# Second product of chunks 1 to 5 with 20 block products in place of 14 per chunk of larger ones, x kept in DRAM, and a new written order

## The chip, the cores and the metric

The kernel runs on one core of one Trainium2 chip. Its time is the device time of one execution in microseconds (us), lower is better; "the median" is that of the executions shown. A profile is one further execution, taken by the hardware profiler. The engines are PE (TensorE: matmuls, with PEld for its weight loads), DVE (VectorE), ACT (ScalarE), POOL (GpSimd) and SP (SyncE, which issues nearly all DMAs).

## The reference

Two parts follow each other. A gated linear recurrence over 4 batches, 8 heads, 768 positions and head size 48, and then a channel MLP with layer normalisation over the 384 values of a position:

```python
for t in range(S):
    state = alpha[:, :, t, :, None] * state + np.einsum('bhd,bhe->bhde', k[:, :, t], v[:, :, t])
    y[:, :, t] = np.einsum('bhd,bhde->bhe', q[:, :, t], state)
x = y.transpose(0, 2, 1, 3).reshape(B, S, H * D)          # (4, 768, 384)
xn = (x - mean(x)) / np.sqrt(var(x) + 1e-06) * g_ln
out = x + np.maximum(xn @ w_ch1, 0.0) @ w_ch2             # w_ch1 384 x 1536, w_ch2 1536 x 384
```

Token tensors are float32; the gain and the weights come as 64-bit floats and are turned to float32 on the chip.

## The kernel before

The 768 positions are cut in 6 chunks of 128 (c = 0 to 5), and all 4 batches (b) of a chunk are worked in parallel. There are these streams of work, each a Python generator that issues one step per turn:

- `attention(c, b)`, 24 of them: logarithm and running sums of the gates (ACT, PE), scaled q and k in the tiles `qks[b]` and `eqs[b]` (DVE, POOL), transposes, masked products (`at`), the output `yps`, the copy of it to `x` (line 290), the state update with the gate row (SP moves one row to DRAM and back, lines 241 and 273), statistics, `xn`, and its transpose into `xT`.
- `take_weights(i)`, 12 pieces: 768 KB are loaded in the tiles `ws` and converted by DVE and ACT.
- `mlp()`: for chunk 0 the plain products (`hidden`, `project`, lines 337 and 349). For chunks 1 to 5 both products are replaced by block schemes that need fewer products and more sums. The first product (`hidden_product`, line 510) uses 15 block products for 18, in the order `FIRST`, twice per chunk (r = 0, 1). The second (`product`, line 404) treats two batches at a time: 7 products of 6 matmuls each in place of 8, so 14 products and 84 matmuls per chunk, each with a moving operand of 192 columns. Every matmul in float32 appears in the trace as two records of PE (two passes).
- `combine_x`, `combine_hidden` (line 390: 4 sums of 128x768 per pair of batches, on DVE), `combine_first` and `combine_weights` (lines 462 and 369, sums of blocks of the weights, on POOL, once), and `relus` (line 562, ACT).

After each product of line 404 its PSUM tile is read: by one DVE or ACT instruction of 128x192, products 5 by two; some results go on to sums on POOL (lines 413, 422, 423, 427). These PSUM tiles (`ops`, `hps`) share the tag "m" with three buffers: the fourth product must wait until the first one has been read. The result tile `ob` (three buffers) starts from `x`, which waits in SBUF in nine buffers, and `send` (line 566) writes it out.

The order of all this is written out by hand in the string `ORDER`: one letter per turn (a to x the attentions, A to L the weight pieces, M the MLP, S the sums of the weights, R relus, X `combine_x`, N `combine_hidden`). Each engine works through its own queue strictly in this order, and so does SP with its DMAs.

Of the kernel before, what the change touches and what calls it, by code (L numbers as in the profile page):

```python
# [22 lines left out]

ORDER = (
    "ababdaacbaabccaabacdacbaabadcbbbdcdAabbbdaBcCccdabAeddbcbdcffcdfeegacfcbagdhfbde"
    "adbceBeegAdhfBCfdeabdfefcAheiBeafdeagjgbecfebcfcgeegfdefdgcghhihfdcgdegCCigMhMgD"
    "DhMjEMEjFMhiDkhfMgfighFheMFFfMMIMEIhIDMgEjhMGhMgjMhgfMGiHMMGGkMMMMHeiJMkMlHJMigM"
    "IMLJilHljMejKKjiLKeLjMhhfjSigSMhMlSMglSlhgiffMKkMhMhSSSMSSSMXiXkikXSXiimjMXXXSSM"
    "MXkMMSkjMMXkMkMMSMMjMmMMjXkmMSlmiMSMMiMkMMXkMjMMMlMlmRMmMMMokSjlMlMnlMnMljnkMMMR"
    "MjnMMMMSMMmMnMMmnRMMRRMoRSkiMlpklniMkpnjmMMRMmMRpkMRMNMMNmMlMiRkmMMiNMMnloMpRMSM"  # L30
    "njNMMkplMoRMMMkMMNmjNMMlMMNNmonnMljomqMMlqMMlnXMMXMXmXnXXMXqMMMXmmXMMooMMMMpMpMn"
    "MMXMMoMoMMMrMoXMnRqoRmoMpMMrpMMMMMMpMMpRnproMMmMMmqMMMrMMMqqMsMMnMnMpJqrRnqsMorM"
    "tMMMMmqMooRppMpotsRMMtRMtMrMRqMRNMoMNMRNMMrMpRMoNsMqMspqpMoMtMMRMMMNMNMMNMMMoMpn"
    "MpNsrrnMtrpqvrquXrXXrXMquXqXsMXsrMXrMqMMXMXuMMMMrMrMLMsMtXMMstMMMtqMsstMMMMMqvRR"
    "MMvMsuMsMtuMMRMMMrMMuwMMMMRMMMvwMvqMttqMMMruRMMRMMsMMRMMMMRMssRtwtsvutxvMRNsvMNN"
    "tMvNsRtRMMMvMtMMuusMMtMMwuuMrMMwwxNxMxvrtNNMMMNMMMtxsMMMuXMXXXMvMvuuXxXXMXvXuMMM"
    "MwwXwMMxMMxMXMMMMMMuvMMxMMuMMwRxMMMwwRMvMwMMMRxuxwxwwMuxMRxvMwMMMxxMMMMMRMMvMMuM"
    "RMMMvMMMxMMRuMRMMRMMNMMMNRMMNMMvMMNMMMwwMMvwMxxRNwRMMNMNNMMMMwxMMvxMXXXXXXMMMMXX"
    "XMMMMMMMMMXMMMMMMMMXMMMMMRRMMMMMMMMMMMMMRMMRMMMMMMMMMMRRMMMRMMRMMMMMMRMNMMMNRNMM"
    "MMNMMMMMMMRMNRMNMMNMMMMNMMMMMMMM"  # L40
# [4 lines left out]
def kernel(  # L45
# [85 lines left out]
    g_col = cpool.tile([P, NF], FP32, name="g_col")  # L131
# [63 lines left out]
    eps = cpool.tile([P, 1], FP32, name="eps")  # L195
    nc.vector.memset(eps, EPS)
    least = cpool.tile([P, 1], FP32, name="least")
# [3 lines left out]
    eqs = [cpool.tile([P, NP, 2, 64], FP32, name=f"eq{b}") for b in range(B)]  # L201
    qks = [cpool.tile([P, 2, NP, 2, 64], FP32, name=f"qk{b}") for b in range(B)]
# [5 lines left out]


# [4 lines left out]
    g20 = cpool.tile([P, NF], FP32, name="g20")  # L214
# [6 lines left out]
    def attention(c, b):  # L221
        qk = qks[b].rearrange("p i a b c -> p i (a b) c")
        eq = eqs[b].rearrange("p a b c -> p (a b) c")[:, :, :D]
# [14 lines left out]
        if c + 1 < NCB:  # L238
            row = dram.tile([1, NP, P], FP32, name="row", tag="row")
            gate = work.tile([P, NP], FP32, name="gate", tag="gate", bufs=B)  # L240
            nc.sync.dma_start(row, eqs[b][P - 1:P].rearrange("o a b c -> o a (b c)"))
# [6 lines left out]
        for i in range(2):  # L248
            tps = ps.tile([R, NP, P], FP32, name="tps", tag="a", bufs=3)
            for p in range(NP):  # L250
                nc.tensor.transpose(  # L251
                    tps[:, p], qks[b][:, i, p].rearrange("p a b -> p (a b)")[:, :R], ident)
            yield
            if i == 0 or c < 2:
                nc.scalar.copy(out=qkT[:, i], in_=tps)
            else:
                nc.vector.tensor_copy(out=qkT[:, i], in_=tps)
            yield
# [30 lines left out]
        x_of[c, b] = x = work.tile([P, DM], FP32, name="x", tag="x", bufs=9)  # L289
        nc.scalar.copy(out=x, in_=yps.rearrange("p a b d -> p (a b d)"))  # L290
        yield
        if c + 1 < NCB:
            sps = ps.tile([R, NP, D], FP32, name="sps", tag="s")
            heads = list(enumerate((slice(0, 64), slice(64, R))))
            for p in range(NP):
                for i, s in heads:
                    nc.tensor.matmul(sps[s, p], qks[b][:, 1, p, i, :s.stop - s.start],  # L297
                                     vt[:, 2 * p + i], start=True, stop=True)
# [32 lines left out]

    def hidden(c, j):
# [10 lines left out]
    ops_of = {}  # L343

    def project(c, b, js):
# [6 lines left out]
        if js[-1] == NJ - 1:  # L352
            ob = work.tile([P, DM], FP32, name="ob", tag="ob", bufs=3)
            nc.vector.tensor_add(ob, ops_of.pop(b), x_of.pop((c, b)))
            nc.sync.dma_start(out[b, c * P:(c + 1) * P], ob)
# [3 lines left out]
    HJ, HM = NJ // 2, DM // 2  # L359
    win = {}  # L360

    def combine_weights():
        b11, b12 = w2[:, :HJ, :HM], w2[:, :HJ, HM:]
        b21, b22 = w2[:, HJ:, :HM], w2[:, HJ:, HM:]
        t1, t2, t4 = (t[:, :HJ * HM].rearrange("p (a c) -> p a c", c=HM) for t in spare)
        ready = win["b"] = {1: b11, 2: b21, 3: b22}
        for n, o, x, y in ((5, t1, b12, b11), (6, t2, b22, t1), (4, t4, b21, t2),
                           (7, b12, b22, b12)):
            nc.gpsimd.tensor_sub(o, x, y)
            ready[n] = o  # L370
            yield

    def quarters(c, b):
        if (c, b) not in win:
            hT = hT_of[c]
            a11, a12, a21, a22 = (hT[:, js, i] for i in (b, b + 1)
                                  for js in (slice(0, HJ), slice(HJ, NJ)))
            win[c, b] = {1: a11, 2: a12, 4: a22}, a21
        return win[c, b]

    def combine_hidden(c, b):
        ready, a21 = quarters(c, b)
        a11, a12, a22 = (ready[n] for n in (1, 2, 4))
        s2, s3, s4 = (work.tile([P, HJ, P], FP32, name=f"sum{i}", tag=f"sum{i}", bufs=1)
                      for i in range(3))
        for n, op, o, x, y in ((7, nc.vector.tensor_sub, s3, a11, a21),
                               (5, nc.vector.tensor_add, a21, a21, a22),
                               (6, nc.vector.tensor_sub, s2, a21, a11),
                               (3, nc.vector.tensor_sub, s4, a12, s2)):
# [4 lines left out]
    def product(c, b, n):  # L394

        if n == 1:
            for i in (0, 1):
                win["o", i] = work.tile([P, 2, HM], FP32, name="ob", tag="ob", bufs=3)
            u = [work.tile([P, 512], FP32, name="u", tag=f"u{i}", bufs=1) for i in range(2)]
            for i in range(4):  # L400
                win["u", i] = u[i // 2][:, i % 2 * HM:][:, :HM]
        acc = ps.tile([P, HM], FP32, name="ops", tag="m", bufs=3)
        for j in range(HJ):
            nc.tensor.matmul(acc, quarters(c, b)[0][n][:, j], win["b"][n][:, j],  # L404
                             start=(j == 0), stop=(j == HJ - 1))
        yield
        x0, x1 = (x_of[c, i].rearrange("p (s m) -> p s m", s=2) for i in (b, b + 1))
        o0, o1 = win["o", 0], win["o", 1]
        p1, u2, u3, u4 = (win["u", i] for i in range(4))
        add, add_late = nc.vector.tensor_add, nc.gpsimd.tensor_add  # L410
        if n == 1:
            nc.scalar.copy(out=p1, in_=acc)
            add_late(o0[:, 0], p1, x0[:, 0])
        elif n == 4:
            add(o1[:, 0], acc, x1[:, 0])
        elif n == 2:
            add(o0[:, 0], acc, o0[:, 0])
        elif n == 6:
            add(u2, acc, p1)
        elif n == 7:  # L420
            add(u3, acc, u2)
            add_late(o1[:, 1], u3, x1[:, 1])  # L422
            add_late(o1[:, 0], u3, o1[:, 0])
        elif n == 5:
            add(u4, acc, u2)
            add(o1[:, 1], acc, o1[:, 1])
            add_late(u4, u4, x0[:, 1])
            send(c, b + 1, o1)
        else:
            add(o0[:, 1], acc, u4)  # L430
            send(c, b, o0)
            del x_of[c, b], x_of[c, b + 1]
# [5 lines left out]
    HB, NT = B // 2, NJ // 3  # L438
# [28 lines left out]
    def combine_x(c):  # L467
# [3 lines left out]
        for i in range(2):  # L471
            t = work.tile([P, HJ, P], FP32, name=f"sum{i}", tag=f"sum{i}", bufs=1)
            t = t.rearrange("p a t -> p (a t)")
            new += [t[:, k * HB * P:(k + 1) * HB * P] for k in range(3)]
        t100, t101, t103 = (t[:, HJ * HM:][:, :HB * P] for t in spare)
        t102, m7, m8, m9, m10, m13 = new
# [15 lines left out]
    FIRST = (3, 7, 5, 10, 9, 1, 4, 14, 11, 6, 13, 2, 8, 0, 12)  # L492

    def hidden_product(c, r, n):
# [38 lines left out]
        elif n == 14:  # L533
            add(u2, acc, u2)
            add_late(c0, u0, u2)
        elif n == 6:
            add(c4, acc, c4)
        elif n == 11:
            nc.scalar.copy(out=c1, in_=acc)
            add_late(c0, c0, c1)  # L540
# [24 lines left out]
    def send(c, b, ob):  # L565
        nc.sync.dma_start(out[b, c * P:(c + 1) * P], ob.rearrange("p s m -> p (s m)"))

    def mlp():
        for c in range(NCB):
# [12 lines left out]
            for b in range(0, B, 2):  # L582
                for n in (1, 4, 2, 6, 7, 5, 3):
                    yield from product(c, b, n)

    spare = []

    def sums():
        for _ in range(3):
            spare.append(stage.tile([P, NF, 2 * P], INT64, name="ws", tag="ws")  # L590
                         .rearrange("p a c -> p (a c)").bitcast(FP32))
# [7 lines left out]
              "N": (x for c in range(1, NCB) for b in range(0, B, 2)  # L599
                    for x in combine_hidden(c, b))}  # L600
# [32 lines left out]
```

## Time and profile before

| quantity | value |
|---|---|
| median of 3 executions | 475.4 us (474.47 to 475.61) |
| the profiled execution's own time, its span | 473.87 us, 471.8 us |
| PE busy, records | 459.0 us (97%), 3712 |
| DVE busy | 327.1 us (69%) |
| POOL busy | 203.8 us (43%) |
| ACT busy | 152.0 us (32%) |
| granted PE clock | full in all slices |
| DMA | 33.84 MB, 72 GB/s mean; mean share of the 16 engines over 0.8 in the first 40 us and 0.2 or less in most slices after 85 us |

An execution's time stands about 2 us above its span. A busy PE is not PE at its peak, since the ends of matmuls are modelled; the starts of neighbouring records show what one really takes.

### The profile page before, as it was taken

The numbers are of one execution on the slowest core, as the hardware profiler recorded it, in microseconds if no ns is written. First come the engines' busy times: TensorE is split into PE (matmuls) and PEld (weight loads), VectorE is DVE, ScalarE is ACT, GpSimd is POOL, SyncE is SP. The second block draws the span as 40 slices with busy tenths as digits, with TensorE's granted clock in tenths as the row PEclk, the third lists the DMA queues.
The fourth block names the chain that finished last, engine by engine and source line by source line (L and its number), as shares of the span: only waits on it lengthen the run. The fifth ranks groups of instructions, "written<-read, shape, count | busy, mean of one in ns | idle before, by whom it ended". The sixth has DMA issues, their size and how long they took to land.

```text
span 471.8 us, 9234 instructions
## 1 busy us (share of the span) xinstructions
PE 459.0 (97%) x3712; PEld 388.5 (82%) x3712; DVE 327.1 (69%) x571; ACT 152.0 (32%) x325; POOL 203.8 (43%) x203
## 2 busy tenths in 40 slices
PE   5989999999999999999999999999999999999997
PEld 3758654566788899988899998899998899987996
DVE  4899997768456985567768378685656576675742
ACT  5676533421132631114341133351203331123300
POOL 5034010049779873127553116573214281145611
PEclk9999999999999999999999999999999999999999
DMA  8988365203112102030211320120010000000000
GB/s 267 334 234 265 78 192 173 83 23 113 52 36 67 35 18 84 8 114 18 86 35 35 100 71 17 35 85 1 33 36 1 1 1 17 18 33 2 0 35 33
DMA packets 32498, 33.84 MB, mean 72 GB/s; under 512 B 13108, under 2 KB 28596, under 8 KB 32456
## 3 DMA queue, kind: packets, MB, share of 16 engines
q1 hardware_dynamic: 31912, 33.12, 22.8%
q8 instruction: 29, 0.48, 0.4%
q10 hardware_dynamic: 544, 0.13, 0.1%
q14 instruction: 13, 0.11, 0.1%
HBM read 28.49 MB, written 4.76 MB: 70 GB/s over the span
## 4 chain that ended last, share of the span: by engine, by line
PE 90%; DMA 4%; DVE 2%; POOL 2%; ACT 2%; SPq 0%; issue 0%; POOLq 0%; DVEq 0%
PE ops L404 29%; PE hps L510 26%; PE hps L337 7%; PE ops L349 7%; PE aps L264 5%; PE yps L286 4%; PE yps L281 4%; PE tps L251 3%; PE lps L228 2%; PE sps L297 2%; PE xps L325 2%; DMA rk<-in_k_dram 2%; DMA ws<-in_moe_w_ch_dram 1%; DMA ra<-in_alpha_dram 1%; DVE w L163 1%; ACT ws L169 0%
## 5 line engine op out<-in xcount | busy, mean ns | idle before, releaser
L307 POOL TENSOR_TENSOR st<-st,gate 128x384 f32<-128x384 f32 x20 | 20.6, 1034 | 76.7 <-issue 30.6
L510 PE MATMUL hps<-sum,w 128*128 128x256 f32 x200 | 51.7, 381 | 0.0
L404 PE MATMUL ops<-w,hT 128*128 128x192 f32 x240 | 42.5, 327 | 0.0
L404 PE MATMUL ops<-w,sum 128*128 128x192 f32 x240 | 42.4, 326 | 0.0
L404 PE MATMUL ops<-ws,hT 128*128 128x192 f32 x240 | 42.3, 326 | 0.0
L562 ACT ACTIVATE hT<-hT 128x512 f32<-128x512 f32 x60 | 36.6, 632 | 16.5 <-POOL hT L548 6.6
L510 PEld LDWEIGHTS hps<-sum,w 128*128 128x128 f32 x200 | 37.1, 190 | 5.2
L404 PEld LDWEIGHTS ops<-w,hT 128*128 128x128 f32 x240 | 39.3, 190 | 0.7
L404 PEld LDWEIGHTS ops<-w,sum 128*128 128x128 f32 x240 | 39.3, 190 | 0.3
L404 PEld LDWEIGHTS ops<-ws,hT 128*128 128x128 f32 x240 | 39.3, 190 | 0.0
L268 DVE COPY_PREDICATED at<-consts,aps 128x512 f32<-128x512 int32 x48 | 32.2, 724 | 10.2 <-PE aps L264 9.9
L286 PE MATMUL yps<-rv,at 128*64 128x48 f32 x768 | 36.4, 219 | 0.0
L422 POOL TENSOR_TENSOR ob<-u,x 128x192 f32<-128x192 f32 x10 | 6.9, 686 | 67.6 <-issue 42.8
L235 POOL TENSOR_TENSOR qk<-rk,ek 128x384 f32<-128x384 f32 x24 | 26.7, 1113 | 19.5 <-ACT ek L232 19.5
L286 PEld LDWEIGHTS yps<-rv,at 128*64 128x64 f32 x768 | 33.0, 137 | 1.3 <-issue 0.7
L529 POOL TENSOR_TENSOR hT<-hT,u 128x512 f32<-128x512 f32 x10 | 12.8, 1284 | 48.6 <-DVE u L528 48.5
L337 PE MATMUL hps<-xT,w 128*128 128x512 f32 x72 | 32.6, 598 | 0.0
L349 PE MATMUL ops<-w,hT 128*128 128x384 f32 x96 | 32.3, 488 | 0.0
L510 PE MATMUL hps<-xT,w 128*128 128x256 f32 x120 | 31.2, 383 | 0.0
L251 PE MATMUL tps<-consts,qk 128*112 128x128 f32 x192 | 29.2, 281 | 1.5 <-DVE at L268 1.0
L264 PE MATMUL aps<-qkT 48*128 48x128 f32 x384 | 28.6, 285 | 1.5 <-DVE at L268 0.8
L251 PEld LDWEIGHTS tps<-consts,qk 128*112 128x112 f32 x192 | 22.8, 137 | 8.8 <-issue 4.1
(127 smaller groups left out, 956.2 us busy)
## 6 DMA issues: line engine op xcount, KB each, us to landing
ws<-in_moe_w_ch_dram SPq DMA_DIRECT2D x12, 768.0 KB
ra<-in_alpha_dram SPq DMA_DIRECT2D x24, 192.0 KB
rk<-in_k_dram SPq DMA_DIRECT2D x24, 192.0 KB
rq<-in_q_dram SPq DMA_DIRECT2D x24, 192.0 KB
rv<-in_v_dram SPq DMA_DIRECT2D x24, 192.0 KB
out_dram<-ob SPq DMA_DIRECT2D x24, 192.0 KB
row<-eq SPq DMA_DIRECT2D x20, 2.0 KB
gate<-row SPq DMA_DIRECT2D x20, 2.0 KB
```

Of the source, the lines that this page charges most:

```text
L235: nc.gpsimd.tensor_mul(qk[:, 1, :, :D], raws.pop(("k", c, b)), ek)
L251: nc.tensor.transpose(tps[:, p], qks[b][:, i, p].rearrange("p a b -> p (a b)")[:, :R], ident)
L264: nc.tensor.matmul(aps[i][:, p], qkT[rows, 1, p], qkT[rows, 0, p], start=True, stop=True)
L268: nc.vector.copy_predicated(out=at[:, i], data=aps[i], mask=mask.unsqueeze(1).broadcast_to([P, NP, P]))
L281: nc.tensor.matmul(yps[s, p].rearrange("p a b -> p (a b)"), qkT[:, 0, p, s], sts[b][:R, p].rearrange("p a b -> p (a b)"), start=True, stop ...
L286: nc.tensor.matmul(yps[s, p, i], at[:, i, p, s], vt[:, 2 * p + i], start=(c == 0), stop=(c == 0 or i == 1))
L307: nc.gpsimd.tensor_mul(st, st, gate.unsqueeze(2).broadcast_to([P, NP, 2 * D]))
L337: nc.tensor.matmul(hps, w1[:, f, j * P:(j + 1) * P], xT_of[c][:, f], start=(f == 0), stop=(f == NF - 1))
L349: nc.tensor.matmul(ops_of[b], hT_of[c][:, j, b], w2[:, j], start=(j == 0), stop=(j == NJ - 1))
L404: nc.tensor.matmul(acc, quarters(c, b)[0][n][:, j], win["b"][n][:, j], start=(j == 0), stop=(j == HJ - 1))
L510: nc.tensor.matmul(acc[:, i], w, b, start=True, stop=True)
L562: nc.scalar.activation(out=x, in_=x, func=AFT.Relu)
```

## The change

Per chunk 1 to 5 the second product is computed for all 4 batches at once. Its left side is cut in 4 x 3 blocks (batches by thirds of the 12 row blocks of w2), its right side in 3 x 2 (thirds by halves of the columns), and a scheme with 20 products of 4 matmuls takes the place of 24. Per chunk these are 80 matmuls for 84, each of the same shape.

- `combine_hidden` has 16 sums of 128x512 per chunk (before: 8 of 128x768). `combine_weights` has 13 sums of 128x768 (before: 4 of 128x1152); four of the results go to a new tile `more`.
- Per chunk, PSUM is read by 24 DVE and 4 ACT instructions of 128x192 (before: 14 and 2), and POOL has 10 sums of 128x192 (before: 8).
- `x` has three buffers; each x is written to DRAM (`kept`, a new step of `attention`) and read back into `ob` (four buffers, new stream `outputs`, letter O). These are 48 more DMAs of 192 KB on SP.
- To make room, `eqs` and `qks` of batches 2 and 3 lie in `more` and are used for chunks 0 and 1 alone, where `more` is not needed yet; from chunk 2 on two `eqs` and three `qks` (b % 2, b % 3) serve all batches. Temporary results of `combine_x` move from `ws` to the `sum` tiles.
- The order of products begins with those whose left blocks need no sum: `SECOND` with 3, 18, 10, 14, and `FIRST` now with 11.
- `ORDER` is a new string.

```diff
-    eqs = [cpool.tile([P, NP, 2, 64], FP32, name=f"eq{b}") for b in range(B)]
-    qks = [cpool.tile([P, 2, NP, 2, 64], FP32, name=f"qk{b}") for b in range(B)]
+    more = cpool.tile([P, 4, NJ // 3 * DM // 2], FP32, name="more")
+    shared = more.rearrange("p i m -> p (i m)")[:, :4 * NP * P]
+    eqs = [cpool.tile([P, NP, 2, 64], FP32, name=f"eq{b}") for b in range(2)]
...
+    def eq_of(c, b):
+        return eqs[b if c < 2 else b % 2]
+    def qk_of(c, b):
+        return qks[b if c < 2 else b % 3]
...
-        x_of[c, b] = x = work.tile([P, DM], FP32, name="x", tag="x", bufs=9)
+        x = work.tile([P, DM], FP32, name="x", tag="x", bufs=3)
         nc.scalar.copy(out=x, in_=yps.rearrange("p a b d -> p (a b d)"))
         yield
+        x_of[c, b] = kept = dram.tile([P, DM], FP32, name="kept", tag="kept", bufs=4 * B)
+        nc.sync.dma_start(kept, x)
+        yield
...
+    def outputs():
+        for c in range(NCB):
+            for b in range(B):
+                ob_of[c, b] = ob = work.tile([P, DM], FP32, name="ob", tag="ob", bufs=B)
+                nc.sync.dma_start(ob, x_of.pop((c, b)))
+                yield
+    def send(c, b):
+        nc.sync.dma_start(out[b, c * P:(c + 1) * P], ob_of[c, b])
...
     def combine_weights():
...
+        for ns, op, o, x, y in (
+                ((8,), add, t8, b[1], b[5]), ((12, 18), sub, t12, b[4], b[5]),
+                ((1, 19), sub, t1, b[2], b[3]), ((9,), sub, t9, b[1], b[3]),
+                ((6,), add, n6, t9, b[5]), ((), add, b[3], b[0], b[4]),
+                ((3,), sub, b[5], b[3], b[2]), ((16,), sub, b[3], b[3], t8),
+                ((2,), add, n2, t9, b[4]), ((5,), add, n5, t9, b[2]),
+                ((10,), sub, n10, b[0], n5), ((0,), sub, n0, t8, b[2]),
+                ((13,), sub, n13, t8, b[4])):
...
+    def combine_hidden(c):
+        a, ready = blocks_of(c)
+        n0, n2, n6, n9, n5, n13 = (
+            work.tile([P, NT, P], FP32, name=f"sum{i}", tag=f"sum{i}", bufs=1) for i in range(6))
+        add, sub = nc.vector.tensor_add, nc.vector.tensor_sub
+        for n, op, o, x, y in (
+                (15, add, a[1], a[0], a[1]), (None, sub, n6, a[2], a[5]),
...
+                (None, add, n5, n5, a[6]), (7, sub, n5, n5, n13)):
+            op(o, x, y)
+            ready[n] = o
+            yield
+    SECOND = (3, 18, 10, 14, 15, 11, 2, 19, 0, 1, 6, 12, 5, 9, 8, 4, 17, 13, 7, 16)
+    def product(c, n):
...
+        acc = ps.tile([P, HM], FP32, name="ops", tag="m", bufs=3)
+        lhs, rhs = blocks_of(c)[1][n], win["b"][n]
+        for j in range(NT):
+            nc.tensor.matmul(acc, lhs[:, j], rhs[:, j], start=(j == 0), stop=(j == NT - 1))
+        yield
...
+        elif n == 18:
+            sub(o(1))
+            sub(o(3))
...
+        elif n == 13:
+            add(q4)
+            late(o(5), q4)
+            late(o(5), g, "sub")
+            late(r8, q4, "sub")
+            late(o(7), r8)
+            late(o(6), r8)
         elif n == 7:
+            add(o(5))
+            send(c, 2)
         else:
+            add(o(6))
+            send(c, 3)
...
-    FIRST = (3, 7, 5, 10, 9, 1, 4, 14, 11, 6, 13, 2, 8, 0, 12)
+    FIRST = (11, 3, 7, 5, 10, 9, 1, 4, 14, 6, 13, 2, 8, 0, 12)
...
             add(u2, acc, u2)
             add_late(c0, u0, u2)
+            add_late(c0, c0, c1)
...
             nc.scalar.copy(out=c1, in_=acc)
-            add_late(c0, c0, c1)
```

Here `add` and `sub` of `product` are DVE instructions that read the PSUM tile, `late` is a POOL instruction, and `o(k)` is half k % 2 of the result tile of batch k // 2.

## The prediction

> **What bounds the kernel now.** I read the page first (busy shares, chain), then PE's waits, then the chain in order of time over the last 60 us, then the product stages as windows.
>
> ```profile
> span 471.8 us, 9234 instructions
> PE 459.0 (97%) x3712; PEld 388.5 (82%) x3712; DVE 327.1 (69%) x571; ACT 152.0 (32%) x325; POOL 203.8 (43%) x203
> PE 90%; DMA 4%; DVE 2%; POOL 2%; ACT 2%; SPq 0%; issue 0%; POOLq 0%; DVEq 0%
> ...
> PE lps L228 <- ACT la L225: 5.4, 3, 4.3
> PE tps L251 <- DVE at L268: 1.0, 2, 0.6
> PE hps L510 <- DVE hT L553: 1.0, 1, 1.0
> ```
>
> PE idles for 471.8 - 459.0 = 12.8 us: 8.5 before 40 us (31.52 of 40 busy there), 1.0 in one place near the end, and 3.3 behind the last matmul. From 40 us on PE is one unbroken queue, so what PE has to do is the time, as long as the other engines keep ahead of it.
>
> ```profile
> 414.02 6.06 PE hps L510 x28
> 420.10 0.70 DVE hT L531
> 420.93 1.27 POOL hT L532
> 422.20 1.42 POOL hT L535
> 423.69 1.28 POOL hT L540
> 425.04 1.27 POOL hT L545
> 426.42 1.27 POOL hT L548
> 427.69 1.24 POOL hT L549
> 428.95 0.70 DVE hT L553
> 429.70 11.49 PE hps L510 x52
> 441.19 27.32 PE ops L404 x168
> ```
>
> This is the chain's end, start and length in us. 168 records of line 404 take 27.32 us: 0.1626 us each. The POOL rows are the 1.0 us wait: six sums without a gap, then L553, whose read sets a PSUM buffer free. In earlier chunks attention work lies between and hides this.
>
> ```profile
> 168.35:203.15 34.80, 34.80 (x313) 33.76 (x312) 22.16 (x43) 6.95 (x17) 14.66 (x14) 1.00 0.13 40
> 243.30:278.97 35.67, 35.67 (x332) 34.63 (x332) 24.43 (x48) 7.11 (x18) 10.04 (x13) 1.00 0.17 51
> 316.00:351.60 35.60, 35.60 (x317) 34.31 (x315) 23.91 (x46) 6.56 (x17) 9.15 (x12) 1.00 0.11 38
> 385.70:414.00 28.30, 28.30 (x179) 28.23 (x178) 19.11 (x38) 4.55 (x12) 7.02 (x10) 1.00 0.06 20
> ...
> L390 DVE TENSOR_TENSOR sum<-hT x20: 947/959/2002, 166.0 to 456.2; 128x768 f32<-128x768 f32 x20
> ```
>
> The windows are the second-product stages of chunks 1 to 4 (window, mean length; then busy PE, PEld, DVE, ACT, POOL; clock; DMA). PE is full; DVE is at 64, 68, 67 and 68%. The last line gives minimum, median and maximum ns of a sum of `combine_hidden`.
>
> **The sum, part by part**, against the profiled execution (473.87 us; its span 471.8 and 2.1 around it). The median shown, 475.4, lies 1.5 above it, so I carry the difference over.
>
> *Matmuls.* Per chunk 84 become 80, two records each: 5 x 4 x 2 = 40 records fewer, of the same shape: 40 x 0.1626 = -6.5 us. All of it is on PE's queue. The product boundaries rise from 14 to 20 a chunk, but 12, 24, 72 and 168 records in a row have taken 1.95, 3.90, 11.70 and 27.32, so a boundary costs nothing by itself.
>
> *DVE in the product stages.* Reads of PSUM: 24 x 0.354 (the 128x192 rows, 0.348 to 0.356) in place of 14: +3.5 us a chunk. Sums: a 128x256 sum takes 0.42, a 128x768 one 0.95 undisturbed, so 128x512 lies at 0.685; the 40 rows of L390 together are 43.2 us, 1.08 each, 14% over 0.95, so 0.78. 16 x 0.78 - 8 x 1.08 = +3.9. Together +7.4 a stage, while PE's share falls by 1.3: 29.6 of 33.5, 31.8 of 34.4, 31.3 of 34.3 and 26.5 of 27.0 us (88, 92, 91, 98%), and in the last chunk (13.13 of 27.6 before) 20.5 of 26.3. The cover is DVE's idle third, and it is nearly used up. Besides, a product is now 8 records, 1.30 us, for 1.95; with three buffers the read must be done within 2.6 us of a product's end, before 3.9. Back-to-back DVE rows start 0.08 earlier than their durations say (L425 at 466.57 with 0.36, L426 at 466.85), so 98% is nearer 93%. Bounds: 0 (all hidden) to 8 us (every stage late by 2). I take +0.5: on average there is room, in an order that puts sums between the reads.
>
> *The last chunk*, where no attention hides anything. (1) In `FIRST`, product 11 now goes first, so 9 and 4, which start POOL's six sums, come one product later (16 records of L510 took 3.46: 0.87 a product); `c0 + c1` still stands in the chain. The gap of 1.0 at 429.7 becomes 1.9: +0.87. Lower bound 0, if POOL's gaps before L532 take it up. (2) At the end of the second half POOL's last sum ended at 443.67 (1.98 long beside a DVE sum, elsewhere 1.24 to 1.28), L553 at 444.40, 3.4 us behind the first record of L404; nothing waited, as its buffer was wanted 3.9 behind. Now the buffer is wanted by the third product at 2.6; 3.4 + 0.87 - 0.7 (undisturbed sum) = 3.55: +0.95, bounds 0 and 1.65. DVE waits in its queue there for POOL, with the first sums and the read of product 3 behind it. (3) After product 13, POOL makes five sums (L423 rows start 0.55 apart) before 16's result can be added: 0.15 + 0.36 + 5 x 0.55 + 0.1 = 3.4 behind 13's end, where the last matmul ends 2.6 and its read would begin at 2.75: +0.65, bounds 0 and 1.0. The DMA behind the last sum stays as it is (2.8 us).
>
> *POOL before chunk 1's products.* 13 sums of 128x768 at 2.63 x 2/3 = 1.75 for 4 at 2.63 to 3.33. Eleven are needed by the third product (10): 19.3 us where three, 7.9, stood: +11.4. From 126.7 to 169.5 POOL idled for some 10 us (5.16, 0.62, 1.16, 0.27, 2.86). PE's new order puts attention between the first and the third product: twice the 16 records of `aps` (1.09 each), one `lps` (0.65), one `yps` block (38.85 to 40.48: 1.63) and three transposes (0.33), 4.8 us. Bounds 0 and 4; I take +0.5.
>
> *DMAs and memory.* 24 + 24 DMAs of 192 KB: 9.4 MB more on engines that are at 0.06 to 0.17 in the stages above. A batch's x is read into `ob` after the earlier result in that buffer has left (2.8 us) and before the next second product, with a first-product stage of 26 us between: hidden. They stand in SP's queue with the loads of a, k, q, v and the gate rows, and some wait for a result; those wait on their part for nothing within tens of us, and SP's queue already waits up to 47 us for results (L566) without a loss for PE. In the first 40 us, where the DMA engines are at 0.89, four x are 0.8 MB, 2.8 us at 282 GB/s, behind the loads that PE then waits for. `x` in three buffers and `eq`/`qk` in two and three make ACT and POOL wait for transfers and reads of one or two batches earlier, with the relus and PSUM copies behind them. The new start of `ORDER` takes batch 1 first (its gates landed 0.9 us after batch 0's). For all this I take 0; bounds -1.5 (part of the 2.4 us that PE idles from 20 to 40 us saved) and +2.8.
>
> Sum: -6.5 + 0.5 + 0.87 + 0.95 + 0.65 + 0.5 = **-3.0 us**: 470.9 for a profiled execution, **472.4** for the median.
>
> [...]
>
> **The rivals.** *All covered*: planned orders keep PE fed as before, the last chunk's gaps do not grow, and only the tail's 0.65 is lost: -5.9, 469.5. For it: only 1.0 us of PE idle after 40 us now, with DVE at 77% from 280 to 316 us too (27.85 of 36). Against: the six POOL sums, whose place I can count.
>
> *POOL is late in chunk 1*: the third product waits 3 to 4 us for `n10`. For: 11.4 us more work against 10 of idle time, in a stretch where POOL is busy 37.35 of 45 us. Against: other queues lag with it, and attention is put in between. Then about 0: 475.4 to 476.
>
> *DVE becomes the bound of the product stages of chunks 1 to 4* (the case on the slower side). If each sum pays 0.35 over 0.685 in place of 0.1, a stage has 4.1 more: 33.7 of 33.5, 35.9 of 34.4, 35.4 of 34.3, 30.6 of 27.0: 6.4 us late, less the 0.5 counted: +2.9, 478.3. It decides from about 1.2 us lost in each of the four stages on. For it: 98% in chunk 4 and a slack of 2.6. Against: undisturbed sums, and POOL at 9 to 14 us of 35.
>
> *The change does not do what it says*: 40 records fewer are fixed by the program; this I exclude.
>
> **How the numbers follow.** My forecast (471.0 to 473.9): 0.42; all covered 0.18; POOL late 0.18; DVE the bound 0.22. Faster by over 0.3% (below 474.0; 0.3% is about what a measurement can tell): 0.42 + 0.18 = 0.60; same 0.18; slower 0.22. The range goes from all covered with a start 1 us shorter, 468.5, to DVE the bound, 478.5; about 1 in 10 is left out on each side.
>
> **What the profile after would show.** Right: 3632 records of PE for 3712, 800 of them at 0.163; PE's waits at the last chunk's first-product read (about 1.9 and 1) and little else after 45 us; DVE at about 77% of the span; the last DVE sum waiting for POOL. Wrong: PE waits for reads in the product stages of chunks 1 to 4 (DVE the bound); a wait of the third product of chunk 1 for POOL; waits for DMA `ob` or `kept`, or of ACT for `row`, which I count as hidden; an idle share in the first 40 us other than 8.5.

## The result and the profile after

The change makes the kernel no faster. Beside each other on one chip the kernel before took 475.13 us and the kernel after 475.08 (medians of four executions each): ratio 1.000, 95% interval 0.9983 to 1.0017. A longer comparison on another chip, made with the experiments, puts it slightly above: 475.54 against 474.43 us, ratio 1.0018 (1.0009 to 1.0027), 0.4 to 1.3 us more. The forecast was 472.4. The profiled execution took 474.99 us (before 473.87), 473.2 of them span.

The page of the kernel after, its head and its chain:

```profile
span 473.2 us, 9321 instructions
PE 455.0 (96%) x3672; PEld 381.6 (81%) x3672; DVE 354.6 (75%) x661; ACT 154.4 (33%) x335; POOL 224.7 (47%) x222
...
PE 79%; DVE 10%; POOL 5%; issue 2%; DMA 1%; ACT 1%; POOLq 0%; SPq 0%; DVEq 0%; ACTq 0%
```

PE has its 40 records fewer (3672; the 3632 in the prediction was a slip, 3712 - 40 is 3672). But its busy time fell by 4.0 us and not by 6.5, and the span rose. The chain tells why: PE held 90% of it before and holds 79% now; DVE and POOL hold 15% (4 before). The waits of PE in the kernel after (line, what it waited for: us in total, times, longest):

```profile
PE lps L242 <- ACT la L239: 5.6, 2, 4.9
...
PE hps L604 <- DVE sum L580: 1.1, 1, 1.1
PE hps L604 <- DVE hT L647: 1.1, 1, 1.1
...
PE ops L448 <- POOL more L408: 0.8, 1, 0.8
PE hps L604 <- DVE hT L636: 0.7, 2, 0.4
PE hps L604 <- DVE hT L616: 0.6, 1, 0.6
...
PE ops L448 <- DVE u L475: 0.3, 1, 0.3
PE ops L448 <- DVE ob L461: 0.3, 1, 0.3
PE ops L448 <- DVE hT L647: 0.2, 1, 0.2
```

The first line is the start, as before. The eight others lie behind 41 us, where the kernel before had one single wait, of 1.0. A busy record covers part of a wait, so I count what each one costs from record to record: the step between two starts less its usual 0.163 us (second product), 0.216 (first product) or 0.109 (from the last `xps` record to a product, at 328). In order of time:

| place, us | who waits for what | lost, us |
|---|---|---|
| 152.8 | chunk 1, first product: buffer read L616 stands behind DVE's multiplication of q | 0.72 |
| 185.1 | chunk 1: read L475, of product 2, stands behind four sums of `combine_hidden` | 0.44 |
| 197.5 | chunk 1, product 13 waits for the weight sum n13 of POOL | 0.97 |
| 328 | chunk 3, read L461 | 0.44 |
| 413.2 | entrance to the last chunk: product 3 waits for DVE's sums of x | 1.26 |
| 425.7 and 440.7 | read L636 waits for POOL's two sums of c0 | 0.56, 0.49 |
| 429.0 and 444.8 | read L647 waits for the end of POOL's six sums | 1.26, 0.39 |

These are 6.5 us (before: 1.17). The last chunk, in the same view that the prediction showed of before (start, length, what; the first two rows are the entrance, where PE waits for DVE's sums of x):

```profile
414.15 0.43 DVE sum L580
414.63 4.60 PE hps L604 x20
...
421.88 1.27 POOL hT L626
423.15 1.24 POOL hT L629
424.47 1.28 POOL hT L630
425.81 1.27 POOL hT L639
427.20 1.27 POOL hT L642
428.47 1.23 POOL hT L643
429.72 0.70 DVE hT L647
430.47 5.46 PE hps L604 x24
```

From 421.88 on it is the same chain of POOL sums, but L629 and L630 now stand in a row behind product 14, and DVE's read L636 needs both. Behind the last matmul the tail grew from 3.31 to 4.15 us, and PE's idle time before 41 us from 8.48 to 8.98.

The product stages of chunks 1 to 4 and the last one (window, length; then busy PE, PEld, DVE, ACT, POOL; clock; DMA) show DVE at 82 to 90% in the first four and 70% in the last, and PE short of full by 0 to 1.1 us:

```profile
165.00:205.00 40.00, 38.91 (x348) 36.12 (x347) 34.53 (x67) 9.56 (x25) 26.15 (x23) 1.00 0.25 76
245.00:280.00 35.00, 35.00 (x329) 32.97 (x328) 28.75 (x64) 6.86 (x18) 11.14 (x14) 1.00 0.16 48
316.00:350.00 34.00, 33.73 (x277) 32.18 (x277) 30.52 (x61) 6.44 (x18) 12.27 (x15) 1.00 0.12 36
385.00:414.00 29.00, 28.53 (x178) 27.96 (x176) 24.40 (x56) 6.99 (x19) 8.48 (x11) 1.00 0.12 38
442.00:468.00 26.00, 25.77 (x158) 25.43 (x157) 18.21 (x40) 2.99 (x8) 6.72 (x9) 1.00 0.05 16
```

### The profile page after: what moved, and what is told of

It reads as the page before. It is cut to its first block, busy times and chain, and to the rows that moved or that the text cites. A ratio compares the mean times of both kernels' runs of the same rounds, so it can differ in the third digit from the quotient of the medians.

```text
span 473.2 us, 9321 instructions
## 1 busy us (share of the span) xinstructions
PE 455.0 (96%) x3672; PEld 381.6 (81%) x3672; DVE 354.6 (75%) x661; ACT 154.4 (33%) x335; POOL 224.7 (47%) x222
## 4 chain that ended last, share of the span: by engine, by line
PE 79%; DVE 10%; POOL 5%; issue 2%; DMA 1%; ACT 1%; POOLq 0%; SPq 0%; DVEq 0%; ACTq 0%
PE hps L604 24%; PE ops L448 22%; PE hps L365 7%; PE ops L377 7%; PE aps L278 4%; PE yps L300 3%; PE yps L295 3%; PE tps L265 3%; PE lps L242 2%; PE sps L314 2%; DVE at L282 2%; PE xps L342 1%; DVE sum L435 1%; POOL ob L464 1%; DVE st L319 1%
## 5 line engine op out<-in xcount | busy, mean ns | idle before, releaser
L464 POOL TENSOR_TENSOR ob<-ob,u 128x192 f32<-128x192 f32 x40 | 27.5, 696 | 79.3 <-DVE ob L461 55.9
L604 PE MATMUL hps<-sum,w 128*128 128x256 f32 x240 | 59.6, 382 | 1.1 <-DVE hT L647 1.1
L604 PEld LDWEIGHTS hps<-sum,w 128*128 128x128 f32 x240 | 44.6, 190 | 7.6 <-DVE hT L647 1.5
L448 PE MATMUL ops<-w,hT 128*128 128x192 f32 x280 | 49.6, 327 | 0.0
L249 POOL TENSOR_TENSOR qk<-rk,ek 128x384 f32<-128x384 f32 x22 | 24.9, 1135 | 36.9 <-ACT ek L246 25.3
L295 PE MATMUL yps<-st,qkT 112*64 112x96 f32 x320 | 29.8, 257 | 0.0
L448 PE MATMUL ops<-ws,hT 128*128 128x192 f32 x160 | 29.5, 327 | 0.3 <-DVE u L475 0.3
L278 PEld LDWEIGHTS aps<-qkT 48*128 48x128 f32 x384 | 24.1, 187 | 6.6 <-issue 3.2
L448 PE MATMUL ops<-ws,sum 128*128 128x192 f32 x160 | 28.6, 327 | 0.3 <-DVE ob L461 0.3
L448 PEld LDWEIGHTS ops<-ws,hT 128*128 128x128 f32 x160 | 26.5, 190 | 1.2 <-DVE u L475 0.6
L242 PE MATMUL lps<-la,consts 128*128 128x384 f32 x48 | 21.1, 536 | 6.0 <-ACT la L239 5.6
```

The lines of the kernel that those rows point to most:

```text
L242: nc.tensor.matmul(lps[:, :DM], tri, la, start=True, stop=True)
L249: nc.gpsimd.tensor_mul(qk[:, 1, :, :D], raws.pop(("k", c, b)), ek)
L278: nc.tensor.matmul(aps[i][:, p], qkT[rows, 1, p], qkT[rows, 0, p], start=True, stop=True)
L295: nc.tensor.matmul(yps[s, p].rearrange("p a b -> p (a b)"), qkT[:, 0, p, s], sts[b][:R, p].rearrange("p a b -> p (a b)"), start=True, stop ...
L448: nc.tensor.matmul(acc, lhs[:, j], rhs[:, j], start=(j == 0), stop=(j == NT - 1))
L464: getattr(nc.gpsimd, f"tensor_{op}")(x, x, y)
```

## The experiments

The theory to test: the 6.5 us are gained on PE's queue and given back in separate waits, each with a place and a cause of its own that can be taken away by itself. The rival: PE's queue is no longer what sets the end; another resource (DVE, the POOL beside it, the DMAs) has the same length, and a wait taken away comes back elsewhere. Times of a set are read against the kernel before on the same chip; single waits are read in the profiles, since PE's idle time in the first 41 us alone differs by more than 1 us between executions of kernels with the same start (8.38 to 9.51 with the start of the kernel after; 8.48 and 10.02 with that of before, in its own profile and in that of g1).

### One wait at a time: e1, e2

```diff
 # e1_n13_early: in ORDER, the last S (weight sum n13) from behind product 9 to behind product 12 of chunk 1
-    "RMSJSiNoMMijoommNpmlMMNMjnOmmkNMnMSMMmkKMMlMNoMNNONNMMmoRMlMMMpMNMMNMMkMpMjmkoNM"
-    "NMNoMSokopNlMMnMMMMMMplOMXXXoMXXoXnnnoXMOmMMMqXMMrMXOXMpMpMMMmrMmMMMMrMMMXMMMMMp"
+    "RMSJSiNoMMijoommNpmlMMNMjnOmmkNMnMSMMmkKMMlMNoMNNONNMMmoRMlMMMpMNMMNMMkMSpMjmkoN"
+    "MNMNoMokopNlMMnMMMMMMplOMXXXoMXXoXnnnoXMOmMMMqXMMrMXOXMpMpMMMmrMmMMMMrMMMXMMMMMp"
 # e2_swap13
-            for n in SECOND:
+            for n in SECOND if c + 1 < NCB else SECOND[:16] + (13, 17, 7, 16):
```

> Only change against the kernel after: POOL's last weight sum, n13, is placed in the written order behind product 12's matmuls of chunk 1 and not behind product 9's. Theory (the 6.5 us are gained on PE and given back in some ten separate waits, each with a place of its own): the 0.97 us wait of product 13 of chunk 1 at 197.5 goes, since POOL idled 9.15 us before 189.0 and n13 itself takes 1.8; the profile shows no wait of PE for L408, and the time falls by 0.97 us, to 474.1. Rival (PE's queue no longer sets the end; DVE, or what it waits for, does): the wait goes and turns up again in the same stage as a wait for DVE; 475.1 as before.

Measured: 474.57 us, ratio to before 0.9992 (0.9981 to 1.0002). PE's wait for L408 is gone, no other took its place, and the last matmul ended at 468.33 for 469.05, although this execution stood 0.34 us later at 46 us (first `aps` record behind 41 us at 46.08 for 45.74). The wait came from the order alone.

> Only change against the kernel after: in the last chunk alone the second products end 4, 13, 17, 7, 16, so that product 13, whose result starts five POOL sums, comes one product (1.30 us) earlier. Theory: the last DVE sum waited 1.41 us for POOL beyond the end of its matmuls; it then waits for PE alone, or nearly so: 0.65 to 1.3 us less, 473.8 to 474.4. Rival: 13's own operand (the DVE sum that feeds it) or the POOL sums of product 9 (L464 rows) are not ready that early, so that PE waits for what the tail saves: 475.1.

Measured: 474.74 us, 0.9999 (0.9990 to 1.0008). The last DVE row, first of the kernel after, then of this one:

```profile
469.98 0.36 DVE L458 TENSOR_TENSOR ob<-ops,ob 128x192 f32<-128x192 f32 x1 [1.41 <-POOL ob L464]
```

```profile
469.53 0.36 DVE L458 TENSOR_TENSOR ob<-ops,ob 128x192 f32<-128x192 f32 x1 [0.94 <-PE ops L448]
```

The last sum no longer waits for POOL, and the tail went from 4.15 to 3.32 us, 0.83 less. (This execution began 0.4 us later, so the span shows 0.5 of it.) Both times are compatible with gains of 0.5 to 1 us, but too close to before to prove them; the profiles do.

### The order of the first product in the last chunk: e3, e4

```diff
+    LAST = FIRST[1:9] + (11,) + FIRST[9:]
+    def old(c, r):
+        return c + 1 == NCB and r in (1,)        # e4: r in (0, 1)
...
-                for n in FIRST:
+                for n in LAST if old(c, r) else FIRST:
...
             add_late(c0, u0, u2)
-            add_late(c0, c0, c1)
+            if not old(c, r):
+                add_late(c0, c0, c1)
...
             nc.scalar.copy(out=c1, in_=acc)
+            if old(c, r):
+                add_late(c0, c0, c1)
```

> Change against the kernel after: in the last chunk's second half alone the products of the first product go 3, 7, 5, 10, 9, 1, 4, 14, 11 and so on, as in the kernel before, with POOL's sum of c0 and c1 behind product 11 again. Theory: POOL's chain of sums begins one product (0.87 us) earlier, and what hangs on it at the entrance to the last second-product stage shrinks: the waits at 440.7 (0.49) and 444.8 (0.39) go, 0.5 to 0.9 us, 474.2 to 474.6. Rival: the order of the products has no part in it (the chain is late because POOL's sums are slower there beside DVE sums): the waits stay, 475.1.

Measured: 474.92 us, 1.0006 (0.9991 to 1.0022), so no gain that the times show. In the profile the losses at 440.7 and 444.8 are gone and the last matmul ended at 468.21, 0.83 earlier than in the kernel after. The pair of waits hangs on the order of the products, as the theory has it.

> As the run with the second half alone, but both halves of the last chunk go in the order of the kernel before. Theory: the waits at 425.7 (0.56) and 429.0 (1.26) fall to the 1.0 of before, 0.8 us less; in return product 3, which waits 1.26 us at 413.2 for DVE's sums of x, now comes first and not second, and its wait grows by up to 0.86. Against the run with the second half alone: between 0.8 less and 0.1 more; 473.4 to 474.7 in all. Rival (FIRST's order is no part of the loss): 475.1 or, with the longer wait for the sums of x alone, 476.

Measured: 476.72 us, 1.0042 (1.0023 to 1.0060): slower than any expectation. Product 3 now came first and lost 2.12 us for 1.26, as expected; what was not expected came behind that pause (windows of this run; the clock is the last but two):

```profile
413.00:415.30 2.30, 0.39 (x3) 0.09 (x1) 2.23 (x6) 0.00 (x0) 1.47 (x3) 1.00 0.24 86
...
416.50:420.20 3.70, 3.70 (x11) 2.94 (x11) 1.34 (x2) 0.59 (x1) 0.00 (x0) 0.54 0.66 208
420.20:421.00 0.80, 0.80 (x5) 0.72 (x4) 0.05 (x1) 0.17 (x1) 0.00 (x0) 1.00 0.00 0
```

For 3.7 us the granted clock was 0.54, and eight records took 0.43 in place of 0.216: 1.7 us more. That did not happen in every execution: eight of the twelve have a mean granted clock of 0.996 or less and took up to 479.20 us; the four at 0.998 and more took 475.13 to 476.11, still above the 474.92 of e3. Of the POOL chain in the first half, the loss at L636 fell to 0.30 and that at L647 stayed at 1.26, where I had expected 1.0. So in the first half the order of the products accounts for 0.26 us; what else delays the chain there this run does not show (DVE's sums of x, L580, stand in front of it in the chains of this run and of the kernel after, and not in that of before). With 11 first in the first half of the last chunk the kernel after is better off, even with the wait that it has there.

### Taking work away: e5, e6, e7

```diff
 # e5_no_late, in product
-            getattr(nc.gpsimd, f"tensor_{op}")(x, x, y)
+            pass
 # e6_no_sums, in combine_hidden (and plain blocks as left operands)
-            op(o, x, y)
-            ready[n] = o
+            pass
 # e7_19
-                yield from product(c, n)
+                yield from product(c, n) if n != 17 else (None, None)
```

> Leaves out of the computation POOL's ten sums of the second product in chunks 1 to 5 (late), so the output lacks those terms; all else stays. Theory (separate waits): the tail behind the last matmul falls from 4.15 to about 2.8, the DVE sums of x at 410 to 413 run at 0.42 and PE's wait there of 1.26 us falls to about the 0.5 that the last copy of xT sets, and part of 0.44 + 0.27 in the product stages goes: 2.3 to 3.0 us less, 472.1 to 472.8. Rival (DVE, held up by POOL on shared memory, sets the end in the product stages of chunks 1 to 4): 1.2 us and more in each of four stages besides, 468 or less, with the L434 sums at 0.69 where they now spread upwards.

Measured: 475.26 us, 1.0014 (1.0001 to 1.0027). Both expectations fall: 50 POOL instructions fewer, and no gain that the times can show. What they paid for themselves went (the wait for n13, the tail from 4.15 to 3.24 us), and something new came (e5, rows of POOL and of DVE in chunk 1):

```profile
183.69 1.02 POOL L249 TENSOR_TENSOR qk<-rk,ek 128x384 f32<-128x384 f32 x1 [3.28 <-ACT ek L246]
184.67 2.26 POOL L408 TENSOR_TENSOR more<-ws,w 128x768 f32<-128x768 f32 x1
...
183.16 0.69 DVE L435 TENSOR_TENSOR sum<-hT 128x512 f32<-128x512 f32 x1
183.88 1.38 DVE L435 TENSOR_TENSOR sum<-sum,sum 128x512 f32<-128x512 f32 x1
185.19 2.29 DVE L435 TENSOR_TENSOR sum<-hT,sum 128x512 f32<-128x512 f32 x1
187.51 0.69 DVE L435 TENSOR_TENSOR sum<-sum,sum 128x512 f32<-128x512 f32 x1
```

In the kernel after POOL idled for 9.15 us at this place, held by a `late` sum that waited for DVE, and the same four sums took 0.69 each:

```profile
182.59 0.69 DVE L435 TENSOR_TENSOR sum<-hT 128x512 f32<-128x512 f32 x1
183.31 0.69 DVE L435 TENSOR_TENSOR sum<-sum,sum 128x512 f32<-128x512 f32 x1
183.92 0.69 DVE L435 TENSOR_TENSOR sum<-hT,sum 128x512 f32<-128x512 f32 x1
184.64 0.69 DVE L435 TENSOR_TENSOR sum<-sum,sum 128x512 f32<-128x512 f32 x1
```

With the `late` sums gone, POOL ran ahead to the gate product and the weight sum n13, and DVE's sums beside them took 1.38 and 2.29: each ended 0.55 us behind the POOL row that it had met (184.71 and 186.93). The four sums stand in front of the read L475, and the 0.44 us that PE lost there became 2.73; a wait of 0.36 for L271 at 336 is new too. At 413.2, where PE's loss fell from 1.26 to 0.17, the sums of x ran at 0.42 to 0.43 us each without POOL; in the kernel after they took up to 0.70.

> Leaves out of the computation the 16 DVE sums of 128x512 per chunk that form the left operands of the second product (combine_hidden); every product takes a plain block of hT, so the output is not the reference's. Theory: PE keeps its queue, DVE loses some 12 us of a stage's 30, and only the waits that the trace puts down to DVE within the product stages go (0.44 at 185.1, 0.27 at 328, some of 0.39 at 444.8): 0.5 to 1.5 us less, 473.6 to 474.6. Rival (DVE is the bound of the product stages): 4 us less or more, 471 or under.

Measured: 473.21 us, 0.9963 (0.9950 to 0.9976), 1.6 us under before; a little more than expected. The losses at 185.1, 197.5 and 328 (1.85 together) are gone, all others stand. DVE lost 53 us of work and the span fell by 1.8: DVE's work is not the bound of these stages.

> Leaves out of the computation product 17 of chunks 1 to 5, its 8 matmul records and its read of PSUM, so the output lacks that term. Theory (PE's queue is the length, waits add at fixed places): 5 x 8 x 0.1626 = 6.5 us less, 468.6, if no wait takes it; the tail behind product 13 then gets 1.3 us longer as only two products follow 13's predecessor as before, so nothing there. Rival (DVE or POOL sets the end of each second-product stage): only the DVE read goes, 5 x 0.35 = 1.8 us less, 473.3; and if what is taken from PE there turns into waits elsewhere, as with the change itself, 475.

Measured: 472.98 us, 0.9948 (0.9930 to 0.9967): 1.9 us under before, though another 40 records are gone. The median is close to the rival's number, but it is not yet what came through. The kernel after stands 0 to 1.1 us above before in the two comparisons, and three of the five executions here ran at a mean granted clock of 0.996; the two at 1.00 took 471.44 and 472.12. In the profile (472.12), from the first `aps` record behind 41 us to the end of the last matmul, PE takes 419.97 us for 423.31 in the kernel after, and the tail is 0.37 shorter: 3.3 of the 6.5 us came through on PE's queue. The rest went into waits, the longest of them here:

```profile
PE ops L448 <- POOL more L408: 2.1, 1, 2.1
```

Product 13 comes 1.3 us earlier without 17, but POOL's n13 does not: its loss grew from 0.97 to 2.27. New waits for DVE's sums (L435) appear, with losses of 0.69 in chunk 2 and 0.66 in chunk 4, and one of 0.26 in the last chunk. So a wait is a moment at which another engine delivers; PE arriving earlier only waits longer there. A gain on PE counts only from the last such moment on. The expectation of 468.6, in which no wait grows, was too simple.

### The transfers alone: e8

```diff
 # the kernel before
         nc.scalar.copy(out=x, in_=yps.rearrange("p a b d -> p (a b d)"))
+        kept_of[c, b] = kept = dram.tile([P, DM], FP32, name="kept", tag="kept", bufs=4 * B)
+        nc.sync.dma_start(kept, x)
...
+        if n == 6:
+            for i in (0, 1):
+                back = work.tile([P, 352], FP32, name="back", tag="back", bufs=1)
+                nc.sync.dma_start(back, kept_of[c, 2 * r + i][:, :352])
```

> The kernel before, with one part of the change alone: each x is also written to DRAM when it is made (24 DMAs of 192 KB), and in chunks 1 to 5 a 128x352 part of it is read back within the first product (20 DMAs of 176 KB); the results still take x from where they did. Theory: the traffic and the places in SP's queue cost nothing, 475.1 within 0.3%, and PE's idle time in the first 40 us stays at 8.5. Rival (the DMAs of x delay the first loads or the loads of a, k, q, v): the 0.5 us that PE idles more in the first 41 us of the kernel after, or more, up to 2.8: 475.6 to 477.9.

Measured: 475.48 us, 1.0018 (1.0003 to 1.0032), 0.6 us over before (0.1 to 1.5). That is at the edge of what can be told. Its profile, 1.8 us longer in span than that of before, shows 8.93 us of idle PE before 41 us, within what executions differ by, one wait of 0.92 at 236.7 for a state sum (L304), which the kernel after does not have, and a tail of 3.60 us for 3.31. Whether x in DRAM costs the kernel after some tenths at its start stays open.

### Removing the waits: f0, f1, f2, f3

f0 is the kernel after, run beside the others of the set. f1 gives two of POOL's six sums in the last chunk to DVE, f2 reorders the sums of x there. f3 is both, with e1 and e2 and two moves in `ORDER` in chunk 1.

```diff
 # f1_dve_sums
-            add_late(c0, u0, u2)
+            (add if c + 1 == NCB else add_late)(c0, u0, u2)
...
-            add_late(c5, c5, u2)
+            (add if c + 1 == NCB else add_late)(c5, c5, u2)
 # f2_x_order, in combine_x
+        if c + 1 == NCB:
+            o = list(order)
+            o[6] = (3, sub, new[9], t101, b[5])
+            order = [o[i] for i in (0, 6, 1, 2, 3, 7, 8, 4, 5, 9, 10)]
 # f3_all, besides: ORDER in chunk 1
-    "ikjjmlMSSMMRMljMMMMSRMnnMMMMkMMkMMMRMMnnlMllllMmmnMMmlpRkkSmMmORMMRjnmMSonmRMRNM"
-    "RMSJSiNoMMijoommNpmlMMNMjnOmmkNMnMSMMmkKMMlMNoMNNONNMMmoRMlMMMpMNMMNMMkMpMjmkoNM"
-    "NMNoMSokopNlMMnMMMMMMplOMXXXoMXXoXnnnoXMOmMMMqXMMrMXOXMpMpMMMmrMmMMMMrMMMXMMMMMp"
+    "ikjjmlMSSMMRMljMMMMSRMnMnMMMkMMkMMMRMMnnlMllllMmmnMMmlpRkkSmMmORMMRjnmMSonmRMRNM"
+    "RMSJSiNoMMijoommNpmlMMNMjnOmmkNMnMSMMmkKMMlMNoMNNOMMNNmoRMlMMMpMNMMNMMkMSpMjmkoN"
+    "MNMNoMokopNlMMnMMMMMMplOMXXXoMXXoXnnnoXMOmMMMqXMMrMXOXMpMpMMMmrMmMMMMrMMMXMMMMMp"
```

> The kernel after once more, beside the three others of this set, so that their small differences are read against it on the same chip: 475.1, as before within 0.2%.

Measured: 475.54 us, 1.0018 (1.0009 to 1.0027). All nine places lose what they lost above, within 0.01 us.

> Change against the kernel after: in the last chunk's two halves of the first product, two of POOL's six sums (c0 = u0 + u2 behind product 14, c5 + u2 behind product 8) go to DVE; POOL keeps four. Theory (separate waits, each with its place): the chain in front of the reads L636 and L647 loses 1.27 us twice, and the waits at 425.7 (0.56), 429.0 (1.26), 440.7 (0.49) and 444.8 (0.39) go, 2.7 us; a DVE sum that meets a POOL sum ended 0.5 us behind it in the run without POOL's sums, which gives 0.4 to 0.8 back: 472.4 to 473.2. Rival (what one wait frees, the next takes): DVE's added sums delay its own reads and PE waits as long at the same places: 475.1.

Measured: 473.69 us, 0.9975 (0.9964 to 0.9985), 1.85 under f0. All four losses went, 2.7 us; the tail took 0.34 of it (4.49 us for 4.15).

> Change against the kernel after: in the last chunk alone DVE makes the sum of x for product 3 second and not seventh (in a free tile of its own), and those for products 7 and 5 before those for 10 and 14. Theory: PE's wait of 1.26 us at 413.2 for that sum goes; it is ready at about 411.3, before product 11 has ended: 473.8 to 474.2. Rival: products 7 or 5 then wait for their sums, which run at 0.54 to 0.70 us beside POOL: half or more of the 1.26 comes back: 474.5 to 475.1.

Measured: 474.49 us, 1.0009 (0.9986 to 1.0032), 1.05 under f0. The loss at the entrance of the last chunk fell from 1.27 to 0.28 us; products 7 and 5 did not wait.

> Change against the kernel after: both of these; product 13 before 17 in the last chunk and n13 early, as in the runs before; and in chunk 1 DVE's multiplication of q (L251) is placed behind the read L616 that waited 0.72 us for it, and two sums of combine_hidden behind the read L475 that waited 0.44 us for them. Theory (the loss is a sum of waits that can be taken away one by one): 0.97 + 0.82 + 2.7 + 1.26 + 0.72 + 0.44 = 6.9 us less, of which contention may keep 1.5: 468.2 to 469.7. Rival (the gain cannot be had, because another resource than PE's queue has the same length): no more than 1 to 1.5 us less, 473.6 or more.

Measured: 469.52 us, 0.9889 (0.9873 to 0.9905): 4.9 us under before and 6.0 under f0, within the 5.4 to 6.9 less that were expected. Page and chain of this kernel, and the last pieces of the chain in order of time:

```profile
span 467.3 us, 9322 instructions
PE 454.6 (97%) x3672; PEld 382.1 (82%) x3672; DVE 356.9 (76%) x665; ACT 155.0 (33%) x335; POOL 221.1 (47%) x218
...
PE 89%; DVE 6%; DMA 2%; ACT 1%; issue 0%; SPq 0%; DVEq 0%; ACTq 0%
```

```profile
411.92 25.69 PE hps L609 x116
437.62 26.01 PE ops L448 x160
```

PE is back at 89% of the chain. From 41.2 us to the end of the last matmul at 463.6 it idles 0.39 us in two gaps, and from 411.92 on it runs without one: the last 160 records take 26.01 us, 0.1626 each. DVE is busier than in the kernel after, and POOL's busy time is less than 2% lower: no engine has had its work reduced by much, the same work only stands elsewhere.

### Whose gain it is: g0, g1, g2

g0 is f3 again, g1 the kernel before with the edit of f1, g2 f3 without product 17 in chunks 1 to 4.

```diff
 # g2_all_19
-                yield from product(c, n)
+                yield from product(c, n) if n != 17 or c + 1 == NCB else (None, None)
```

> The kernel with all seven moves once more, beside the two others of this set: 4.9 us under the kernel before, ratio 0.989.

Measured: 469.50 us, 0.9889 (0.9874 to 0.9905), as before.

> The kernel before, with the same two POOL sums of the last chunk given to DVE. Theory (what the moves are worth depends on the waits that stand in the kernel): the kernel before has one wait of 1.0 us behind 41 us, at 429.7, and that is all that can go: 0.8 to 1.1 us less, ratio 0.998; so the rest of the 4.9 us comes from the 40 records. Rival (the moves are worth as much on the kernel before, and the change is worth nothing by itself): 1.9 us less or more, as on the kernel after.

Measured: 473.39 us, 0.9968 (0.9956 to 0.9980): 1.6 us less (0.9 to 2.1), above the expected 0.8 to 1.1, and the times alone do not exclude the rival's 1.9. The profile does: the wait at 429.7, 1.17 us from record to record, is gone, and behind 41 us PE has no gap left that a move could free; why the times show 1.6 us and not 1.2 stays open. So with no wait left in the kernel before, the change with its moves is still 3.9 us faster (473.39 against 469.50). The moves gave 6.0 us on the kernel after; most of that is the change's own gain, set free.

> The kernel with all seven moves; leaves out of the computation product 17 of chunks 1 to 4 (8 records each), so the output lacks that term there. Theory (where no wait stands behind it, what is taken from PE's queue is time): 32 x 0.1626 = 5.2 us less than the kernel with all moves, of which the two DVE sums of 0.5 us that product 17's absence let PE wait for in chunk 2, and some for n13 in chunk 1, may keep 1.5: 3.7 to 5.2 less, 464.3 to 465.8. Rival (on the kernel after, leaving 17 out in five chunks gave 2 to 2.9 of 6.5, because the product stages have another bound): again 30 to 45 in 100, 1.6 to 2.3 less, 467.2 to 467.9.

Measured: 465.73 us, 0.9810 (0.9795 to 0.9825), 3.8 us under g0 of the 5.2 that the 32 records measure, 72%. Measured in the profiles as for e7, 3.7 us came through (413.72 us for the 417.46 of f3), where on the kernel after it was 3.3 of 6.5, 51%. The wait for n13 does not come back; two for DVE's sums (L435), 0.69 us in chunk 2 and 0.66 in chunk 4, keep most of the rest. That is the expectation of the theory, and far from the rival's 1.6 to 2.3.

## Why the prediction was wrong

The price of the records was right, the direction of the foreseen waits too; what failed was the count of the places. From the two profiled executions, in us of span:

| step of the sum | foreseen | measured |
|---|---|---|
| 40 records of 0.1626 fewer | -6.5 | -6.5 |
| DVE in the product stages | +0.5 | +0.88 (185.1 and 328) |
| POOL's weight sums in chunk 1 | +0.5, at the third product | +0.97, at product 13 |
| (1) last chunk, order of `FIRST` | +0.87 | +0.65 (0.56 and 1.26, less the 1.17 of before) |
| (2) entrance to the last second-product stage | +0.95 | +0.88 (440.7 and 444.8) |
| (3) five POOL sums behind product 13 | +0.65 | +0.84 |
| start | 0 | +0.5 |
| first product of chunk 1, L616 behind L251 | not seen | +0.72 |
| entrance to the last chunk, sums of x | not seen | +1.26 |
| more steps of 0.10 in PE's queue | not seen | +1.2 |

The measured column gives +1.4, and the spans differ by +1.4. The losses that I had priced came to 3.5 us and measured 4.2: sizes, by and large, were right, though single terms are off by up to 0.5 and of (1) e4 ties only 0.26 us to the order. Another 3.7 us came from places that I had set at nothing.

- **"... and little else after 45 us"** is the sentence that failed. I looked for PE's idle places in the trace of before, where there was one, and followed the change through that place alone. But each wait of the kernel after is a read or an operand whose slack had been hidden by PE's longer queue or by the old order; with 1.3 us less per chunk and a new order, the slack was used up in nine places, and PE lost 0.4 to 1.3 us in each. The sums of x at 413.2 were nowhere in the working, though `FIRST` and the last chunk were; and of `c0 + c1` I wrote that it "still stands in the chain", but not that DVE's read of product 2 needs it (L636, 1.05 us in two places).
- **DVE in the product stages**: right. Its sums took 62.0 us for 80, 0.775 each, against the 0.78 taken, and the stages stood at 82 to 90%. The rival "DVE becomes the bound" is refuted by e6. But the average that the term was built on does not place the sums: its two waits come from reads that stand behind sums in DVE's order.
- **"14% over 0.95, so 0.78"** was half right. As an average it held: 63 of the 80 sums took under 0.70. But of the 17 others 16 end 0.55 us behind the end of a POOL row that ran beside them, up to 2.03 for 0.68 us (at 173.17, the POOL row from 172.50 to 174.64). In e5 one took 2.29 for 0.69, and in the kernel after L251, which ends 0.41 behind its POOL row, took 1.77 for 0.55; that is the 0.72 us at 152.8:

```profile
150.83 1.81 POOL L408 TENSOR_TENSOR w<-w 128x768 f32<-128x768 f32 x1
...
151.28 1.77 DVE L251 TENSOR_TENSOR qk<-rq,eq 128x384 f32<-128x384 f32 x1
152.97 0.68 DVE L616 TENSOR_TENSOR hT<-hps,hT 128x512 f32<-128x512 f32 x1
```

  An average over a stage does not show that: it matters where the slow row stands, here in front of a read that PE needs.
- **POOL late in chunk 1**: the rival's total came true by other causes. The third product did not wait for n10 at all; n13 stood late in POOL's order for product 13, behind sums that wait for DVE.
- **Transfers and memory at 0**: nothing behind 41 us waits for `ob` or `kept`, as foreseen. Of the 0.5 us at the start I can't tell a cause from the differences between executions.
- **The steps of 0.10**: in both kernels the first full-size record behind small attention records (`aps`, `yps`, `sps`) takes 0.104 us longer, and so does one behind a wait. Before there are 20 such steps (19 of them behind attention), after 32 (23 behind attention, 9 behind a wait).

What was argued and not shown: that PE's shorter queue, and not the new `ORDER`, uses up each of the slacks; only for n13 does e7 show that PE's arrival sets the length of the wait.

## What to carry to other kernels

Where an engine is busy without a gap, its work is the time only as long as nobody else's due date comes close: before pricing a shorter queue at its full length, list for every operand and every buffer read how long before use it is ready, and take the gain only down to the smallest of these slacks (this kernel suggests it; it was not tried on another). When such a change comes out at nothing, read the waits one by one and move their causes; here seven moves that left nearly all work in place turned 0 into 1.1%. And an average duration hides a collision: look for the single slow row in front of a read.

## What the runs showed of the hardware

Less work on one engine lengthened another's in e5: without 50 POOL sums the kernel gained nothing (1.0014 of the kernel before), because POOL reached a sum of 2.26 us while DVE made its sums of two SBUF operands, and one of these took 2.29 for 0.69. DVE rows with one operand in PSUM kept their time beside POOL (L616: 0.68 at 152.97, while POOL ran L249 from 152.59 to 153.90): in the kernel after all 120 of them of 128x512 took 0.65 to 0.69, and all 120 of 128x192 0.32 to 0.36. Not every sum of two SBUF operands beside POOL was slower (L435: 0.68 at 195.17, while POOL ran two rows of L464 from 194.26 to 196.85); what decides that no run shows.

A pause of PE of 1.96 us was followed by 3.7 us at a granted clock of 0.54 (e4), and one of 2.6 us between 15 and 20 us in g1 by a clock of 0.50 from 22 to 24 us; a pause of 2.57 us in e5 left the clock at 1.00 in the profile. So the clock fell behind such a pause in two profiles of three; what decides that no run shows, and e4's executions differ among themselves (mean granted clock 0.985 to 1.00).
